# Attention beside the first half of d_ff: TensorE in program order, each product a step behind its inputs, pairs made sooner, partial sums over ScalarE's queue

## The chip, the cores and the metric

The kernel runs on one core of one Trainium2 chip. The metric is device time in microseconds, the median of several executions. TensorE (PE in the profile) multiplies matrices, VectorE (DVE), ScalarE (ACT) and GpSimd (POOL) do the elementwise work, and SyncE (SP) starts nearly all transfers. Each engine works through its own queue in order and waits on semaphores for the others.

## The reference

Three pieces are chained. Sizes: 8 batches, 8 heads, 576 positions, head dimension 64, 32 memory slots; 4608 tokens, d_model 512, d_ff 2048, and 768 for the last piece.

```python
a = exp(phi - max(phi, axis=2)); a = a / (sum(a, axis=2) + 1e-9)     # over the sequence
k_m = einsum('bhsm,bhsd->bhmd', a, k);  v_m = einsum('bhsm,bhsd->bhmd', a, v)
attn = softmax(q @ k_m^T / sqrt(D))                                  # over the 32 memory slots
x = attn @ v_m                                                       # to 4608 x 512
h = x @ w_in;  g = h - tanh(h);  x = g @ w_out                       # 512 -> 2048 -> 512
out = max(x @ w1, x @ w2, x @ w3) @ w_out2                           # 512 -> 768 -> 512
```

## The kernel before

The change touches the first piece and the first half of the second, roughly the first 490 of 1364 us. fp32 products are made of two parts, a high and a low one, so a product is three matmuls (`mm3`).

**The main line.** d_ff is split in 16 chunks of 128, and phase 0 does chunks 0 to 7, phase 1 the others. The list `steps` has one entry for each token tile and chunk: steps 0 to 31 are four tiles of 288 tokens (chunks 0 to 3 of all four, then chunks 4 to 7 of all four), and from step 32 on come tiles of 320, 512 and 320 tokens with eight steps each, so that phase 0 has 104 steps. A step i, in `run`, emits the twelve matmuls of `emit_x(i)` (four output blocks ps_x, gh against wo), after the first block the elementwise work of step i + 3 (`emit_g`: tanh, subtraction, and the split into gh), and after all blocks `emit_h(i + 4)`, the products ps_h. x @ w_in is folded: h is attn times vw, where vw = v_m @ w_in is made for each batch and each quarter of d_ff. When a tile's chunks end, its sums go out of ps_x into xo and to DRAM (xd). For the first four tiles the sums of chunks 0 to 3 are stored, loaded into xo at chunk 4 of the second round, and added to ps_x at chunk 7. xo has a single buffer, and the next tile's first ps_x product waits until its bank has been emptied.

**The side line.** Meanwhile the attention of later batches is made, by generators which `slot()` advances five times in each step, at a fixed rate. `Track fg` holds them in a list, each with a gate, the step from which it may begin. For a batch b there are: `kv_gen` (maxima mx of phi, transposed on TensorE into ps_mx; a diagonal dg multiplied by ones, to spread the maximum; subtraction from phi; Exp; the products ps_kv; n; the transposition ps_t into kT and vT), two `q_gen` (transposes qT of q; products sc; the softmax chain s, st on four engines; aT and at) and two `vw_gen` (products ps_w with vT and wi, cast and subtraction into vw). These eight products a batch share two PSUM banks, m0 and m1, each held until VectorE has taken its contents out. The gates stand relative to `start[0, b]`, the first step that needs the batch (8, 32, 40, 56, 64, 80 and 88 for batches 1 to 7): kv 20 steps ahead, q 16, vw 8 and 6. If `emit_h` needs something that isn't made, `Track.need` runs the list up to it at once.

**The order.** All instructions go through `Paced.call` (line 57 in the profile). The framework's scheduler then places each engine's instructions by its own estimate of time, and not in the order of the code. `behind(ins, mark)` is a bond of order only, without a semaphore: an instruction of the side line stays behind the last tanh, subtraction or x product of the main line that was emitted ahead of it. Transfers go over SyncE's queue, `DMA = nc.sync`.

Of the kernel before, what the change touches and what calls it, by code (L numbers as in the profile page):

```python
# [22 lines left out]
def kernel(  # L23
# [22 lines left out]
    nc = tc.nc  # L46

    class Paced:

        def __init__(self, engine):  # L50
            self.engine, self.mark = engine, None

        def __getattr__(self, name):
            op = getattr(self.engine, name)

            def call(*a, **kw):
                i = op(*a, **kw)  # L57
                if self.mark is not None and background[0]:
                    behind(i.ins, self.mark)
                return i  # L60

            return call
# [20 lines left out]
    LG = 3  # L83
# [146 lines left out]
    def phi_gen(b):  # L230
        load_phi(b)
        ph = phi_t.pop(b)
        yield
        mx = ap.tile([P, H, M], F32, tag="mx", bufs=1, name="mx")
        V.tensor_max(mx, ph[:, :, 0], ph[:, :, 1])
        for c in range(2, C):
            V.tensor_max(mx, mx, ph[:, :, c])
        yield
        pm = bank(1, [P, 2, 2, P], "ps_mx")
        for i in range(2):  # L240
            T.transpose(pm[:, 0, i], mx[:, 4 * i:4 * i + 4].rearrange("p h m -> p (h m)"), ident)
        mt = ap.tile([P, 2], F32, tag="mt", bufs=1, name="mt")
        V.tensor_reduce(mt, pm[:, 0], axis=AX.X, op=ALU.max)
        yield
        dg = ap.tile([P, 2, P], F32, tag="mx", bufs=1, name="dg")
        V.tensor_tensor(out=dg, in0=ident[:, None, :].to_broadcast([P, 2, P]), in1=mt[:, :, None].to_broadcast([P, 2, P]), op=ALU.mult)
        T.matmul(pm[:, 1].rearrange("p i j -> p (i j)"), ones, dg.rearrange("p i j -> p (i j)"), start=True, stop=True)
        yield
        freed[1] = V.tensor_tensor(out=ph, in0=ph, in1=pm[:, 1].rearrange("p i (h m) -> p (i h) m", m=M)[:, :, None, :].to_broadcast([P, H, C, M]), op=ALU.subtract).ins
        yield  # L250
        S.activation(ph, ph, AF.Exp)
        yield
        ph_t[b] = ph
        yield

    vT = [wi_p.tile([P, HP, M], F32, name=f"vT{b}") for b in range(B)]
    kT = {}
# [2 lines left out]
    def kv_mm(b):  # L260
        ph = ph_t.pop(b)
        ps = bank(0, [P, 2, 256], "ps_kv")
        t = kv_t.pop(b)
        for e in range(2):
            for c in range(C):
                pk = P if c < 4 else 64
                for r in range(HP):
                    T.matmul(ps[32 * r:32 * r + 32, e, 2 * D:2 * D + 1], ph[:pk, 2 * r + e, c], ones[:pk, :1], start=c == 0, stop=c == C - 1)
            for c in range(C):
                pk = P if c < 4 else 64  # L270
                for r in range(HP):
                    T.matmul(ps[32 * r:32 * r + 32, e, :2 * D], ph[:pk, 2 * r + e, c], t[:pk, :, 2 * r + e, c], start=c == 0, stop=c == C - 1)
                if c % 2:
                    yield
            yield
        if b:
            load_phi(b + 1)
            load_kv(b + 1)
        rc = ap.tile([P, 2], F32, tag="rc", bufs=2, name="rc")
        V.tensor_scalar(rc, ps[:, :, 2 * D], 1e-9, None, ALU.add)  # L280
        V.reciprocal(rc, rc)
        n = ap.tile([P, 2, 2, D], F32, tag="kvn", bufs=2, name="n")
        V.tensor_tensor(out=n.rearrange("p i e d -> p e i d"), in0=ps[:, :, :2 * D].rearrange("p e (i d) -> p e i d", i=2),
                        in1=rc[:, :, None, None].to_broadcast([P, 2, 2, D]), op=ALU.mult)
        yield
        pt = bank(0, [P, 2, P], "ps_t")
        for i in range(2):
            for e in range(2):
                T.matmul(pt[64 * e:64 * e + 64, i], n[:, i, e], ident, start=True, stop=True)
        kT[b] = ap.tile([P, HP, M], F32, tag="kT", bufs=2, name="kT")  # L290
        for i, t in enumerate((kT[b], vT[b])):
            S.copy(t.rearrange("p r m -> p (r m)"), pt[:, i])
        yield
# [8 lines left out]
    def q_gen(b, hfs):  # L302
# [6 lines left out]
        for hf in hfs:  # L309
            qT = []  # L310
            for g in range(2):
                t = ap.tile([P, 2, NH], F32, tag="qT", bufs=2, name="qT")
                V.transpose(out=t, in_=q_t[b, g][:, :, hf * JH:(hf + 1) * JH].rearrange("p r j d -> p r (j d)"))
                qT.append(t)
                yield
            scs = [bank(e, [P, NH], "sc") for e in range(2)]
            small([(scs[e][32 * r:32 * r + 32], kT[b][64 * e:64 * e + 64, r], qT[r // 2][64 * e:64 * e + 64, r % 2])
                   for r in range(HP) for e in range(2)])
# [32 lines left out]
    vw_t = {}  # L351

    def vw_gen(ph, b, fq):
        while 2 * ph + fq not in wi:
            bg.need("wi2")
        t = at_p.tile([P, 2, 2, FQ], F32R, tag="vw", bufs=4, name="vw")
# [66 lines left out]
        yield  # L423


    class Track:
        def __init__(self):
            self.q = []

        def add(self, name, g, gate=-1):  # L430
            self.q.append([name, g, gate])

        def step(self, now):
            if self.q and self.q[0][2] <= now:
                try:
                    next(self.q[0][1])
                except StopIteration:
                    self.q.pop(0)
                    self.step(now)
# [78 lines left out]
    def emit_g(i):  # L518
        ps = h_t.pop(i)
        nt = steps[i][1][1]  # L520
        th = ga_p.tile([P, NT], F32, tag="th", bufs=2, name="th")[:, :nt]
        S.mark = S.activation(th, ps, AF.Tanh).ins
        V.mark = V.tensor_sub(th, ps, th).ins
        gh = ga_p.tile([P, 2, NT], F32R, tag="gh", bufs=4, name="gh")[:, :, :nt]
        S.copy(gh[:, 0], th)
        G.tensor_sub(gh[:, 1], th, f(gh[:, 0]))
        g_t[i] = gh
# [6 lines left out]
    def emit_x(i):  # L534
# [6 lines left out]
            emit_x.ps = [ps_x.tile([P, NT], F32, tag=f"x{dm}", bufs=1, name=f"ps_x{dm}")[:, :nt] for dm in range(KD)]  # L541
        o = slice(t0, t0 + nt)
        add = ph or t0 < NXI and fc >= 4
        if fc == 4 and add or final and not add:
            emit_x.xo = ga_p.tile([P, KD, NT], F32, tag="xo", bufs=1, name="xo")[:, :, :nt]
            if add:
                DMA.dma_start(out=emit_x.xo, in_=xd[0][:, :, o])
        for dm in range(KD):
            T.mark = mm3(emit_x.ps[dm], (wt[:, 0, dm * P:(dm + 1) * P], wt[:, 1, dm * P:(dm + 1) * P]),
                (gh[:, 0], gh[:, 1]), first, final)  # L550
# [7 lines left out]
                emit_g(i + LG)  # L558
            slot()
        if final:  # L560
            DMA.dma_start(out=xd[ph][:, :, o], in_=emit_x.xo)

    hooks = {}

    def run(lo, hi):
        for i in range(lo, hi):
            now[0] = i
            for fn in hooks.pop(i, ()):
                fn()
            emit_x(i)  # L570
# [57 lines left out]
    for ph in range(2):  # L628
        for b in range(B):
# [2 lines left out]
            aq = max([s0 - AHEAD + 4] + [last_u[bb - 3, fq] - LG for fq in range(2) if bb > 2])  # L632
            av0, av1 = (max(s0 - d, last_u[order[2 * bb + fq - 4]] - LG) if bb > 1 else 0 for fq, d in enumerate((8, 6)))
            if ph == 0 and b > 1:
                fg.add("kv", kv_gen(b), s0 - AHEAD)
                fg.add(("q", 0, b, 0), q_gen(b, (0,)), aq)
                fg.add(("q", 0, b), q_gen(b, (1,)), aq)
            if ph:
                fg.add(("q", 1, b, 0), at_load(b), max(aq, s0 - 10))
            if bb > 1:  # L640
                fg.add(("vw", ph, b, 0), vw_gen(ph, b, 0), av0)
                fg.add(("vw", ph, b, 1), vw_gen(ph, b, 1), av1)
        if ph == 0:
# [284 lines left out]
```

## Time and profile before

| | |
|---|---|
| median of 3 runs | 1368.9 us (1366.58 to 1371.0) |
| profiled execution | 1365.75 us, span 1364.0 us, mean granted clock 0.985 |
| TensorE matmuls | 1285.4 us busy, 94% of the span |
| VectorE, ScalarE, GpSimd | 751.2, 507.1 and 531.8 us busy |

The span is from the first to the last instruction that the profiler recorded. The stage of the change lies between 104 and 449 us: at 104 us step 9 begins, at 449 us step 92.

### The profile page before, as it was taken

The page shows a single profiled execution, that of the slowest core. Times are in us where ns is not written, and L with a number is a line of the kernel's source. Part 1 is how long each engine was busy: PE and PEld are TensorE (multiplying, and loading weights), DVE is VectorE, ACT ScalarE, POOL GpSimd, SP SyncE. Part 2 cuts the span into 40 slices and gives each one's busy share as a digit, 9 for nine tenths or more (in the row PEclk, how much of TensorE's full clock was granted, in tenths as well). Part 3 has the DMA queues.
Part 4 walks back from the last instruction along what each step waited for, and adds up shares of the span by engine and source line. Part 5 has one row for each costly group of instructions (what it writes and reads, how often), then busy time and mean ns, then how long its engine had stood idle before and what let it go on. Part 6 is the DMA issues. An engine that isn't in the chain of part 4 may idle for free.

```text
span 1364.0 us, 22739 instructions
## 1 busy us (share of the span) xinstructions
PE 1285.4 (94%) x8996; PEld 1157.4 (85%) x8996; DVE 751.2 (55%) x1189; ACT 507.1 (37%) x993; POOL 531.8 (39%) x470
## 2 busy tenths in 40 slices
PE   3578898999998999999999999999999999999998
PEld 1457696897897799898989999999999899999996
DVE  3868557666545755756643344555734546457342
ACT  2446244454334455555544332223322323233221
POOL 1637334554423546776754341132311312223110
PEclk9989998999999899999999999999999999999999
DMA  8874847866714536667575139838557477385431
GB/s 204 243 194 127 207 139 189 215 213 172 186 57 178 189 105 236 242 206 251 207 254 168 50 125 364 342 126 307 192 171 286 141 270 268 97 307 197 166 132 47
DMA packets 188394, 264.94 MB, mean 194 GB/s; under 512 B 94976, under 2 KB 160512, under 8 KB 179200
## 3 DMA queue, kind: packets, MB, share of 16 engines
q1 hardware_dynamic: 188000, 259.82, 58.3%
q0 software_dynamic: 288, 3.67, 0.7%
q8 instruction: 71, 1.16, 0.4%
q14 instruction: 35, 0.29, 0.1%
HBM read 199.49 MB, written 63.96 MB: 193 GB/s over the span
## 4 chain that ended last, share of the span: by engine, by line
PE 84%; DVE 7%; SPq 3%; issue 2%; POOL 2%; ACT 1%; DMA 1%; POOLq 0%; ACTq 0%; DVEq 0%
PE b L57 40%; PE ps_x L57 26%; PE ps_h L57 13%; PE ps_w L57 2%; PE ps_kv L57 2%; DVE cvb L57 2%; SPq L224 1%; DVE st L57 1%; DVE s L57 1%; POOL s L57 1%; DVE mx L57 1%; DMA raw<-in_moe_w_out_dram 1%; SPq L214 1%; DVE th L57 1%; DVE vw L57 0%
## 5 line engine op out<-in xcount | busy, mean ns | idle before, releaser
L57 PE MATMUL ps_x<-gh,wo 128*128 128x320 f32 (+2 forms) x2400 | 451.9, 335 | 7.2 <-DVE xo L57 5.5
L57 PEld LDWEIGHTS ps_x<-gh,wo 128*128 128x128 f32 x2400 | 381.4, 191 | 54.7 <-issue 22.9
L57 PE MATMUL b<-mv,sw 128*128 128x384 f32 x2268 | 401.6, 338 | 0.0
L57 PEld LDWEIGHTS b<-mv,sw 128*128 128x128 f32 x2268 | 399.1, 188 | 1.4 <-DMA sw<-sw_d 0.3
L57 POOL TENSOR_TENSOR gh<-th,gh 128x320 fp32r<-128x320 f32 (+2 forms) x200 | 209.8, 1051 | 259.0 <-ACT gh L57 248.9
L57 PE MATMUL ps_h<-at,vw 128*128 128x256 f32 (+2 forms) x1536 | 254.9, 307 | 20.4 <-DVE th L57 10.0
L57 PEld LDWEIGHTS ps_h<-at,vw 128*128 128x128 f32 x1536 | 227.7, 197 | 47.7 <-DVE th L57 15.6
L57 DVE TENSOR_TENSOR th<-ps_h,th 128x320 f32<-128x320 f32 (+2 forms) x200 | 106.7, 536 | 184.2 <-ACT th L57 183.5
L57 ACT ACTIVATE th<-ps_h 128x320 f32<-128x320 f32 (+2 forms) x200 | 95.2, 478 | 200.2 <-PE ps_h L57 185.7
L57 PE MATMUL b<-wz,mh 128*128 128x512 f32 x648 | 150.4, 390 | 1.1 <-DVE ob L57 1.1
L57 PEld LDWEIGHTS b<-wz,mh 128*128 128x128 f32 x648 | 121.3, 188 | 26.5 <-DVE ob L57 2.0
L57 ACT CAST gh<-th 128x320 fp32r<-128x320 f32 (+2 forms) x200 | 99.6, 499 | 96.0 <-DVE th L57 83.8
L57 POOL TENSOR_TENSOR c<-c,u 128x384 f32<-128x384 f32 x36 | 36.5, 1015 | 226.6 <-ACT u L57 226.6
L57 ACT COPY p<-b 128x384 f32<-128x384 f32 x108 | 51.8, 479 | 169.6 <-PE b L57 146.4
L57 DVE TENSOR_TENSOR c<-b,u 128x384 f32<-128x384 f32 x72 | 39.9, 554 | 97.0 <-PE b L57 97.0
L57 DVE TENSOR_SCALAR cvb<-cvb 128x512 f32<-128x512 f32 x112 | 69.8, 624 | 29.8 <-ACT cvb L57 27.0
L57 DVE TENSOR_TENSOR m<-c,m 128x768 f32<-128x768 f32 x72 | 69.0, 958 | 5.7 <-DVE c L57 0.9
L57 DVE TENSOR_TENSOR c<-b,p 128x384 f32<-128x384 f32 x72 | 37.7, 554 | 37.7 <-ACT p L57 34.2
L57 DVE TENSOR_TENSOR vw<-ps_w,vw 128x512 fp32r<-128x512 f32 x64 | 41.4, 681 | 22.9 <-ACT vw L57 22.9
L57 POOL TENSOR_TENSOR mv<-xr,mv 128x384 fp32r<-128x384 f32 x30 | 48.9, 1664 | 12.4 <-PE b L57 9.3
L57 POOL TENSOR_TENSOR m<-m,u 128x384 f32<-128x384 f32 x18 | 21.4, 1189 | 81.6 <-ACT u L57 80.2
L57 ACT CAST mh<-m 128x384 fp32r<-128x384 f32 (+1 forms) x54 | 31.8, 620 | 57.1 <-DVE m L57 57.1
(82 smaller groups left out, 1051.5 us busy)
## 6 DMA issues: line engine op xcount, KB each, us to landing
sw<-sw_d SPq DMA_DIRECT2D x52, 1792.0 KB, 7.6
sw_d<-so SPq DMA_DIRECT2D x9, 1792.0 KB, 7.1
raw<-in_moe_w_out_dram SPq DMA_DIRECT2D x22, 512.0 KB, 5.5
qt<-in_q_dram SPq DMA_DIRECT2D x128, 72.0 KB, 3.1
at_d<-at SPq DMA_DIRECT2D x16, 576.0 KB, 3.7
at<-at_d SPq DMA_DIRECT2D x8, 1152.0 KB, 6.3
raw<-in_moe_w_dram SPq DMA_DIRECT2D x18, 512.0 KB, 4.0
out_dram<-ob SPq DMA_DIRECT2D x144, 64.0 KB, 1.7
```

Of the source, the lines that this page charges most:

```text
L57: i = op(*a, **kw)
L214: DMA.dma_start(out=t[:64, i, :, 4], in_=x[b, :, 4 * P:].rearrange("h p d -> p h d"))
L224: q_dma.dma_start(out=t[64 * e + 32 * h:64 * e + 32 * h + 32, r], in_=src[e, h, r])
```

## The change

It has four parts. (1) From step 9 to step 91, `T.strict` puts every TensorE instruction behind the one emitted before it, so TensorE works in the order of the code. (2) A generator of the side line yields `turns(b)` ahead of a product, and `Track.step` then leaves it alone until that many tanh have been emitted: two until step 28, then one, none for batches 0 and 1. (3) The list of the side line is in another order, with other gates: batches come in pairs (2 and 3, 4 and 5, 6 and 7), the second kv of a pair and its first vw ahead of the first batch's second vw, and most gates are the step in which the buffers that are needed come free, instead of a fixed distance ahead of their use. (4) In phase 0 the stores of xo, and the loads of the four tiles' sums, are started from ScalarE's queue. A load is emitted at chunk 5 instead of 4, and behind the last tanh emitted.

```diff
@@ Paced.call
+                if self.strict:
+                    if self.prev is not None:
+                        behind(i.ins, self.prev)
+                    self.prev = i.ins
@@ phi_gen, kv_mm, q_gen, vw_gen: ahead of ps_mx, dg x ones, ps_kv, ps_t, sc and ps_w
-        yield
+        yield turns(b)
@@ Track
+    turn = [0]
+    def turns(b):
+        return 0 if b < 2 else 2 if now[0] < start[0, 2] - 4 else 1
...
-                    next(self.q[0][1])
+                    if self.q[0][3] < turn[0]:
+                        n = next(self.q[0][1])
+                        self.q[0][3] = turn[0] + n - 1 if n else -1
@@ emit_g
+        turn[0] += 1
@@ emit_x
-        if fc == 4 and add or final and not add:
+        if fc == (4 if ph else 5) and add or final and not add:
...
-                DMA.dma_start(out=emit_x.xo, in_=xd[0][:, :, o])
+                d = (DMA if ph else nc.scalar).dma_start(out=emit_x.xo, in_=xd[0][:, :, o]).ins
+                if ph == 0:
+                    behind(d, S.mark)
...
-            DMA.dma_start(out=xd[ph][:, :, o], in_=emit_x.xo)
+            (DMA if ph else nc.scalar).dma_start(out=xd[ph][:, :, o], in_=emit_x.xo)
@@ run
+            T.strict = 8 < i < start[0, B - 1] + 4
@@ the list of the side line
-                fg.add("kv", kv_gen(b), s0 - AHEAD)
+                if b % 2 == 0:
+                    fg.add("kv", kv_gen(b), s0 - AHEAD)
+                    aq = max([s0 - AHEAD] + [last_u[bb - 3, 1] - LG for _ in range(b > 2)])
+                else:
+                    aq = last_u[bb - 3, 1] - LG
+                av0, av1 = (last_u[order[2 * bb + fq - 4]] - LG for fq in range(2))
+                if b % 2:
+                    fg.add(("vw", 0, b - 1, 1), vw_gen(0, b - 1, 1), last_u[order[2 * bb - 5]] - LG)
                 fg.add(("q", 0, b, 0), q_gen(b, (0,)), aq)
                 fg.add(("q", 0, b), q_gen(b, (1,)), aq)
+                fg.add(("vw", 0, b, 0), vw_gen(0, b, 0), av0)
+                if b % 2:
+                    fg.add(("vw", 0, b, 1), vw_gen(0, b, 1), av1)
+                else:
+                    fg.add("kv", kv_gen(b + 1), av0)
```

**Where instructions stand, before and now.** The first place is TensorE where the vw of batch 3 are made; ps_w with vT_92 are their two products, each with all heads. In the kernel before, this is at the end of step 39 (wo_962 and wo_963 are the weights of chunks 6 and 7, and with wo_304 and 512 tokens step 40 begins):

```order
L57 MATMUL ps_x_2149<-gh,wo_963 128x320 x3
L57 MATMUL ps_x_2150<-gh,wo_963 128x320 x3
L57 MATMUL ps_x_2151<-gh,wo_963 128x320 x3
L57 MATMUL ps_x_2152<-gh,wo_963 128x320 x3
L57 MATMUL ps_w<-wi,vT_92 32x512 x8
L57 MATMUL ps_h<-at,vw 128x256 x10
L57 MATMUL ps_w<-wi,vT_92 32x512 x8
L57 MATMUL ps_h<-at,vw 128x256 x2
L57 MATMUL ps_mx<-ident,mx 128x128 x2
L57 MATMUL ps_h<-at,vw 128x256 x12
L57 MATMUL ps_x_2571<-gh,wo_304 128x512
```

Now the same two products stand in steps 36 and 37 (wo_957 and wo_958 are the weights of chunks 4 and 5):

```order
L57 MATMUL ps_x_2049<-gh,wo_957 128x320 x3
L57 MATMUL sc<-qT,kT 32x288 x8
L57 MATMUL ps_x_2050<-gh,wo_957 128x320 x3
L57 MATMUL ps_x_2051<-gh,wo_957 128x320 x3
L57 MATMUL ps_x_2052<-gh,wo_957 128x320 x3
L57 MATMUL ps_h<-at,vw 128x256 x6
L57 MATMUL ps_w<-wi,vT_92 32x512 x8
L57 MATMUL ps_h<-at,vw 128x256 x6
L57 MATMUL ps_x_2049<-gh,wo_958 128x320 x3
L57 MATMUL ps_w<-wi,vT_92 32x512 x8
```

Both products have moved ahead of steps 37 to 39, the first into the middle of the h of step 40 and directly ahead of the half that uses it, and ps_mx of the next batch has gone from here to a place behind both.

The second place is TensorE in step 32 now (wo_304 is the weight of chunk 0); ps_t belongs to batch 3, and ps_w with vT_91 is the second product of batch 2. In the kernel before, this ps_w stands some steps earlier, apart from the h that uses it.

```order
L57 MATMUL ps_x_2049<-gh,wo_304 128x320 x3
L57 MATMUL ps_t<-ident,n 64x128 x4
L57 MATMUL ps_x_2050<-gh,wo_304 128x320 x3
L57 MATMUL ps_x_2051<-gh,wo_304 128x320 x3
L57 MATMUL ps_x_2052<-gh,wo_304 128x320 x3
L57 MATMUL ps_w<-wi,vT_91 32x512 x8
L57 MATMUL ps_h<-at,vw 128x320 x6
```

So ps_w now stands between the last product of step 32 and the h of step 36, which is the first to need its vw.

The third place is the load of xo (L547 before, L561 now) and the store (L561 before, L577 now) around steps 23 to 25. Before, they stand on SyncE's queue:

```order
L561 DMA xd_120<-xo 512x1x288
L224 DMA qt<-in_q_dram 32x18x32 x11
L547 DMA xo<-xd_120 128x4x288
L224 DMA qt<-in_q_dram 32x18x32 x4
L344 DMA at_d_1416<-at 512x1x288
```

Now they stand on ScalarE's queue; the first tanh (th) of these rows is that of step 24, the next those of 25, 26 and 27:

```order
L57 ACTIVATE th<-ps_h 128x288
L57 CAST gh<-th 128x288
L57 ACTIVATE th<-ps_h 128x288
L57 CAST gh<-th 128x288
L57 ACTIVATE th<-ps_h 128x288
L561 DMA xo<-xd_120 128x4x288
L57 CAST gh<-th 128x288
L57 ACTIVATE s<-s 128x576
L57 ACTIVATE th<-ps_h 128x288
L57 CAST gh<-th 128x288
L577 DMA xd_120<-xo 512x1x288
```

The load has left its place behind eleven pieces of q, and now stands behind the tanh of step 26 and ahead of those of 27 and later.

## Rows read from the trace of the kernel before

**Rows 1.** Windows: us, busy time of each engine (matmuls), PEclk, DMA share, GB/s.
```profile
104.00:449.00 345.00, 322.63 (x3095) 274.65 (x3096) 209.39 (x372) 148.43 (x301) 156.91 (x144) 0.97 0.59 168
166.00:172.50 6.50, 5.67 (x30) 3.76 (x31) 5.89 (x15) 1.07 (x2) 1.18 (x1) 0.50 0.76 221
220.50:230.50 10.00, 8.09 (x41) 5.59 (x42) 7.07 (x13) 5.37 (x11) 4.28 (x4) 0.51 0.72 220
320.00:330.00 10.00, 6.97 (x65) 4.25 (x64) 7.65 (x14) 6.17 (x12) 3.62 (x3) 1.00 0.84 203
420.00:430.00 10.00, 6.50 (x54) 4.65 (x47) 5.42 (x11) 5.70 (x11) 4.33 (x4) 0.94 0.63 205
428.50:432.50 4.00, 4.00 (x21) 3.94 (x20) 0.69 (x1) 1.78 (x4) 3.08 (x3) 0.57 0.98 339
```

**Rows 2.** Timeline of TensorE: start, duration, instruction, [idle before it, releaser].
```profile
127.40 0.41 PE L57 MATMUL ps_mx<-ident,mx 128*128 128x128 f32 x2 [1.41 <-DVE mx L57]
...
159.88 2.08 PE L57 MATMUL ps_h<-at,vw 128*128 128x288 f32 x12 [0.77 <-DVE th L57]
166.84 1.06 PE L57 MATMUL ps_x<-gh,wo 128*128 128x288 f32 x3 [4.88 <-DVE xo L57]
...
218.10 1.09 PE L57 MATMUL ps_w<-wi,vT 64*32 64x512 f32 x16 [2.20 <-DVE s L57]
221.09 2.56 PE L57 MATMUL ps_h<-at,vw 128*128 128x256 f32 x10 [1.89 <-ACT vw L57]
...
227.59 0.69 PE L57 MATMUL ps_mx<-ident,mx 128*128 128x128 f32 x2 [1.33 <-DVE vw L57]
...
327.70 0.44 PE L57 MATMUL ps_mx<-ident,mx 128*128 128x128 f32 x2 [1.67 <-DVE vw L57]
...
427.59 3.68 PE L57 MATMUL ps_h<-at,vw 128*128 128x256 f32 x20 [2.21 <-DVE th L57]
```

**Rows 3.** Timeline of SyncE's queue: start, duration, instruction.
```profile
150.95 10.57 SPq L224 DMA_DIRECT2D qt<-in_q_dram  x11
161.56 0.63 SPq L547 DMA_DIRECT2D xo<-xd  x1
```

**Rows 4.** Tile xo from 104 to 449 us, its loads and stores.
```profile
DMA to landing us min/median/max: 3.3/4.1/7.1
```

**Rows 5.** Timeline of TensorE, two starts one step of 288 tokens apart.
```profile
142.96 0.97 PE L57 MATMUL ps_h<-at,vw 128*128 128x288 f32 x6
...
145.35 0.29 PE L57 MATMUL ps_h<-at,vw 128*128 128x288 f32 x1
```

**Rows 6.** VectorE's groups, 104 to 449 us: busy us, mean ns, idle before.
```profile
L57 DVE TENSOR_TENSOR vw<-ps_w,vw 128x512 fp32r<-128x512 f32 x28 | 18.2, 677 | 7.5 <-ACT vw L57 7.5
...
L57 DVE SCALAR_TENSOR_TENSOR cvb<-raw,cvb 128x512 uint32<-128x512 uint32 x15 | 15.1, 1007 | 0.2
L57 DVE TENSOR_TENSOR mx<-mx,phi 128x256 f32<-128x256 f32 x18 | 12.9, 717 | 0.3
L57 DVE TENSOR_SCALAR cvb<-cvb 128x512 uint32<-128x512 uint32 x15 | 11.6, 771 | 0.3
...
L57 DVE TENSOR_SCALAR cvb<-cvb 128x512 f32<-128x512 f32 x15 | 9.6, 637 | 5.2 <-ACT cvb L57 4.7 <-POOL cva L57 0.4
L57 DVE STREAM_TRANSPOSE aT<-s 128x576 f32<-128x576 f32 x12 | 9.3, 776 | 10.1 <-POOL s L57 10.1
L57 DVE TENSOR_TENSOR phi<-phi,ps_mx 128x1280 f32<-128x1280 f32 x6 | 8.9, 1481 | 2.4 <-PE ps_mx L57 2.4
L57 DVE TENSOR_TENSOR xo<-ps_x,xo 128x288 f32<-128x288 f32 x16 | 6.4, 447 | 9.5 <-PE ps_x L57 4.8 <-DMA xo<-xd 4.7
```

**Rows 7.** ScalarE's group of the Exp of phi, 104 to 449 us.
```profile
L57 ACT ACTIVATE phi<-phi 128x1280 f32<-128x1280 f32 x6 | 7.7, 1276 | 4.8 <-DVE phi L57 4.8
```

**Rows 8.** Timeline of ScalarE at the start: two casts of vw.
```profile
83.85 1.07 ACT L57 CAST vw<-ps_w 128x512 fp32r<-128x512 f32 x2 [1.74 <-PE ps_w L57]
```

**Rows 9.** Timeline of TensorE behind these casts.
```profile
86.42 0.72 PE L57 MATMUL sc<-qT,kT 64*32 64x288 f32 x16 [1.40 <-DVE vw L57]
```

More of the change, by code (lines that the diff above doesn't have):

```diff
@@ L50, in __init__ @@
         def __init__(self, engine):
-            self.engine, self.mark = engine, None
+            self.engine, self.mark, self.strict, self.prev = engine, None, False, None
         def __getattr__(self, name):
@@ L243, in phi_gen @@
         V.tensor_reduce(mt, pm[:, 0], axis=AX.X, op=ALU.max)
-        yield
         dg = ap.tile([P, 2, P], F32, tag="mx", bufs=1, name="dg")
         V.tensor_tensor(out=dg, in0=ident[:, None, :].to_broadcast([P, 2, P]), in1=mt[:, :, None].to_broadcast([P, 2, P]), op=ALU.mult)
+        yield turns(b)
         T.matmul(pm[:, 1].rearrange("p i j -> p (i j)"), ones, dg.rearrange("p i j -> p (i j)"), start=True, stop=True)
@@ L251, in phi_gen @@
         S.activation(ph, ph, AF.Exp)
-        yield
+        yield turns(b)
         ph_t[b] = ph
-        yield
     vT = [wi_p.tile([P, HP, M], F32, name=f"vT{b}") for b in range(B)]
@@ L284, in kv_mm @@
                         in1=rc[:, :, None, None].to_broadcast([P, 2, 2, D]), op=ALU.mult)
-        yield
+        yield turns(b)
         pt = bank(0, [P, 2, P], "ps_t")
@@ L315, in q_gen @@
                 yield
+            yield turns(b)
             scs = [bank(e, [P, NH], "sc") for e in range(2)]
@@ L353, in vw_gen @@
     def vw_gen(ph, b, fq):
+        if ph == 0:
+            yield turns(b)
         while 2 * ph + fq not in wi:
@@ L430, in add @@
         def add(self, name, g, gate=-1):
-            self.q.append([name, g, gate])
+            self.q.append([name, g, gate, -1])
         def step(self, now):
@@ L543, in emit_x @@
         add = ph or t0 < NXI and fc >= 4
-        if fc == 4 and add or final and not add:
+        if fc == (4 if ph else 5) and add or final and not add:
             emit_x.xo = ga_p.tile([P, KD, NT], F32, tag="xo", bufs=1, name="xo")[:, :, :nt]
             if add:
-                DMA.dma_start(out=emit_x.xo, in_=xd[0][:, :, o])
+                d = (DMA if ph else nc.scalar).dma_start(out=emit_x.xo, in_=xd[0][:, :, o]).ins
+                if ph == 0:
+                    behind(d, S.mark)
         for dm in range(KD):
@@ L634 @@
             if ph == 0 and b > 1:
-                fg.add("kv", kv_gen(b), s0 - AHEAD)
+                if b % 2 == 0:
[6 more added lines that the diff above has]
+                    fg.add(("vw", 0, b - 1, 1), vw_gen(0, b - 1, 1), last_u[order[2 * bb - 5]] - LG)
                 fg.add(("q", 0, b, 0), q_gen(b, (0,)), aq)
                 fg.add(("q", 0, b), q_gen(b, (1,)), aq)
+                fg.add(("vw", 0, b, 0), vw_gen(0, b, 0), av0)
[3 more added lines that the diff above has]
+                    fg.add("kv", kv_gen(b + 1), av0)
             if ph:
                 fg.add(("q", 1, b, 0), at_load(b), max(aq, s0 - 10))
-            if bb > 1:
                 fg.add(("vw", ph, b, 0), vw_gen(ph, b, 0), av0)
```

## The prediction

> **What bounds the kernel now.** I read the windows first, over the stretch in which the change acts: from step 9, at 104 us, to step 92, at 449 us. TensorE is busy for 322.6 of these 345 us [rows 1], so all that a better order can save there is 22.4 us of idle time, and what a lowered clock costs. Both lie in few places. The windows around 325 and 425 us hold 3.0 and 3.5 us of idle time, though ScalarE and VectorE have work for only 5 to 8 us of each ten. In three windows the granted clock is near 0.5 or 0.57, so TensorE runs partly or wholly at 1.2 GHz instead of 2.4 [rows 1]. A matmul at half clock takes twice as long, so a window costs its busy time times the missing share: 5.67 × 0.50 = 2.8 us around 170, 8.09 × 0.49 = 4.0 us around 225, and 4.00 × 0.43 = 1.7 us around 430 us. Each of the three falls stands right behind waits of TensorE.
>
> Next I read TensorE's own timeline at these places, for what it waited for [rows 2]. There are four kinds. (a) The first transposes of batch 2 (ps_mx) wait 1.4 us for VectorE's maxima. (b) At 166.84, in step 24, the input product of partial sums waits 4.9 us for VectorE's additions into xo, after a wait of 0.8 for a late subtraction in the step before, which I count with it. (c) At 218 to 228, in steps 39 and 40, a pair's ps_w, its h and the following ps_mx wait 2.2, 1.9 and 1.3 us. (d) At 327.70 and 427.59 what stands behind two later pairs waits 1.7 and 2.2 us. A bank of m0 or m1 is held there until VectorE has taken its contents out, and vw is asked for the moment that it is made.
>
> For (b), SyncE's queue says what was late [rows 3]: the load of xo leaves at 161.56, behind eleven pieces of q that took the queue 10.57 us to issue. From there to the product that waits it is 166.84 − 161.56 = 5.3 us.
>
> **The change, part by part.**
> *Sums over ScalarE's queue.* The four loads no longer stand behind q's pieces, but the load for step 24 now stands behind the tanh of step 26 (the order shows this), which runs at the start of step 23. A step of 288 tokens takes 145.35 − 142.96 = 2.4 us [rows 5]. With 0.5 us for the tanh, as an estimate, and the 5.3 from issue to product, the product can start at 5.8, where it would be due at 2.4: a wait of 3.4 us in place of 4.9 + 0.8. That gains 2.3 us. A load or store of xo lands in 3.3 to 7.1 us, 4.1 in the middle [rows 4], so the wait lies between 2.6 and 6.4. I take the clock fall behind it (2.8) as staying, since a wait of 3.4 remains. The Trainium skill (DMA: Bandwidth & Descriptors, Issuing engines are not separate DMA queues) says that transfers started by different engines share the same 16 DMA engines, and that another issuer saves only the time to start them, usually little. By that rule alone step 24 would gain nothing and the sum below would be 2.3 us higher, near 1366.8. Here the time to start them was itself the trouble: 10.57 us of issuing ahead of one load.
>
> *Program order and one step between input and product.* A product no longer stands on TensorE until its turn has come, and no later work can go ahead of it. In (a), ps_mx stands a whole step later, so its 1.4 us go. In (d), the second pair of vw for batches 4 and 6 comes several steps earlier, so the idle time of both windows goes, 3.0 + 3.5, and so does the clock fall behind the second, 1.7. Sum: −9.6 us. The bounds are nothing (the waits turn up elsewhere, a rival) and all of it.
>
> In (c), sc and ps_w of batch 3 keep nearly their distance: the order shows a pair of ps_w right behind the first half of h(40) in step 36. I keep its first two waits, 2.2 and 1.9, and halve the third, since ps_mx now stands two steps later: 4.8 instead of 5.4, a gain of 0.6. The bounds are 1.9 and 7.6, one wait alone or every wait with half as much again. The fall (4.0) stays.
>
> *What is new.* Where work is in order and not yet ready, TensorE now stands still. I looked for the products whose VectorE or ScalarE work cannot end in time, by adding the means [rows 6, 7] between two subtractions of tanh.
> Step 28: the order has four maxima, aT, two vw and three additions to xo between two subtractions, 4 × 0.72 + 0.78 + 2 × 0.68 + 3 × 0.45 = 6.4 us, where two steps give 4.8. I take 1.4 for the rest (0 to 4), as the first of the additions frees the first bank early.
> Step 32: the second ps_w of batch 2 is forced out directly ahead of the h that uses it. The copy and the subtraction of one half are 0.53 + 0.68 = 1.2 us [rows 6, 8], and with 0.5 for what the engines are in at that time it is 1.7. The bounds are 0.7 and 3.0, the latter as two halves and hand-overs.
> Step 47: ps_mx of batch 5 shares a bank with vw of batch 4. Between two subtractions VectorE has four maxima, aT, two vw and three passes of a weight's splitting (0.64 + 0.77 + 1.01), 7.4 us, against some two steps of 320 tokens. I take 2.0 (1 to 3).
> The other products, some 44, have a step between input and use. The longest chain is phi's: 1.48 on VectorE and 1.28 on ScalarE [rows 6, 7], 2.8 us where the shortest step gives 2.4. Most steps are longer, so I take 0.05 for each, 2.0 us in all (0 to 11, below).
>
> *The start.* Before step 9, two copies of xo and a store now stand ahead of the casts of vw on ScalarE; TensorE already waits 1.4 us for that vw [rows 9]. Two copies are about 2 × 0.45, as VectorE's operations on such a tile [rows 6], and one issue about 0.6 [rows 3], 1.5 in all; some of it lies beside the ps_w that the casts wait for anyway, so I take 1.0 (0 to 2.2). After step 92 the order of every engine is as before, so those stages cost nothing and give nothing.
>
> *Sum.* Gains: 2.3 + 9.6 + 0.6 = 12.5. Losses: 1.4 + 1.7 + 2.0 + 2.0 + 1.0 = 8.1. Net −4.4 us against the profiled execution of 1365.75 us, which is 1361.35. The median of the runs is 1368.9, a factor of 1.0023 above it, so **1364.5 us**, 0.32% less. A change of 0.3% is about what a measurement of this kernel can tell from none.
>
> **The rivals.**
> *A clean success.* The step between input and product does what it can: the new waits halve (−4), (c) halves too (−2.4) and, without its waits, has no clock fall (−4.0). Net −14.8, so 1354.0 us. For it speaks the stretch's many steps without any wait: TensorE's idle time sits in so few places that most products have slack now. Against it: (c) hangs on a chain through three engines that is as long as before.
> *Slower: one step is too short.* TensorE's free order now lets other matmuls run while a product's input is late; in strict order each late input is TensorE's own idle time. It decides above 0.15 us for each of 44 products (then −4.4 + 44 × 0.10 = 0). At 0.30 each, 0.25 more than I counted, 11 us come onto the sum: +6.6, which is 1375.5 us. For it: phi's chain of 2.8 us against a step of 2.4, and VectorE and ScalarE, each with its own order. Against it: most steps are of 320 or 512 tokens.
> *Slower: the transfers hold ScalarE.* Each store waits for four additions and each load for the landing of the store before it, and behind both stands a tanh. From a store to the load behind it are 4.1 us of landing [rows 4] against 2.4 of a step; the h that needs the bank which this tanh empties comes two steps on, 4.8 us [rows 5], and less some 1.7 for tanh, subtraction and h's own place (an estimate) the lead is 3.1. If each of four tiles loses 2 us beyond that lead, the sum is +3.6, so 1372.5 us; it decides from 1.1 us each. The Trainium skill (TensorE: Matmul & The Clock Gate, Architectural detail: the array is 16× 32×32, not 1× 128×128) calls ScalarE's queue strictly first in, first out, which would hold a tanh behind such a transfer. No row shows a transfer on ScalarE's queue before.
> *The waits only move.* What (a), (b) and (d) give comes back at the next product in order, because the chains through three engines, and not the order, set the total of idle time. Net 0, 1368.9 us. For it: the stages without idle time have little left to hide a chain in. Against it: the three engines besides TensorE are at most three quarters busy in the windows of (d) [rows 1].
>
> **How the numbers follow.** Chances: the forecast 0.42, clean success 0.22, steps too short 0.15, ScalarE held 0.09, waits only move 0.12. The forecast's own range, from 1360 to 1369, comes from the bounds of steps 24, 28 and 36; its middle stands at the edge of 0.3%, so 0.24 of its 0.42 count as faster and 0.18 as the same. Faster: 0.24 + 0.22 = 0.46. The same: 0.18 + 0.12 = 0.30. Slower: 0.15 + 0.09 = 0.24. The range 1350 to 1375 leaves out the slower half of the slow cases (0.12) and the best third of clean success (0.07).
>
> **What would show it.** In the changed profile: the windows around 325 and 425 us of before without idle time; the wait for xo's additions near step 24 at 3.4 us with a fall of the clock behind it; ps_w and h in step 36 with 4 to 5 us of waits and a fall; waits of 1 to 2 us at steps 28, 32 and 47. The sum is wrong if idle time between 104 us and the end of step 92 differs by more than 4 us from 22.4 − 10.8 + 7.1 = 18.7 us (10.8 of the gains are idle time, 1.7 the clock's), or if ScalarE's tanh waits behind a transfer.

## The result, and the profile after

The changed kernel is slower: 1378.49 us median (6 runs, 1375.9 to 1381.28) against 1370.94 us for the kernel before in the same setting (6 runs, 1366.58 to 1371.07), a ratio of 1.0066 with a 95% interval of 1.0048 to 1.0083. The prediction of 1364.5 us and its range up to 1375 are both below it. The profiled execution has a span of 1374.1 us, 10.1 more than before.

First the windows by stage, in the changed kernel: steps 0 to 8, 9 to 43, 44 to 59, 60 to 91, 92 to 103 (columns as in [rows 1]), then one window in the middle of the third stage. A stage begins here with the tanh that its first step emits, which is the tanh of three steps on. By this measure step 9 begins at 113.7 us in the kernel before; at the 104 us named above, TensorE is still in the products of step 8.

```profile
58.60:116.00 57.40, 42.49 (x401) 33.32 (x402) 41.88 (x66) 23.36 (x49) 27.83 (x25) 0.76 0.73 203
...
116.00:260.70 144.70, 129.90 (x1339) 109.18 (x1338) 92.30 (x166) 58.38 (x122) 60.99 (x60) 0.95 0.58 164
260.70:334.50 73.80, 64.59 (x574) 52.18 (x573) 45.65 (x80) 33.25 (x67) 39.37 (x35) 0.93 0.73 204
334.50:462.50 128.00, 127.14 (x1148) 108.36 (x1147) 66.81 (x116) 53.12 (x103) 48.92 (x43) 1.00 0.42 130
...
462.50:504.90 42.40, 39.56 (x249) 33.78 (x247) 24.29 (x37) 18.92 (x41) 19.68 (x19) 1.00 0.47 156
...
324.50:331.30 6.80, 5.56 (x30) 3.89 (x31) 3.81 (x8) 3.41 (x7) 6.00 (x6) 0.50 0.86 183
```

The same stages of the kernel before, by its own times of these tanh:

```profile
58.80:113.70 54.90, 40.81 (x416) 32.07 (x417) 41.22 (x66) 23.38 (x50) 28.62 (x26) 0.88 0.77 209
...
113.70:256.30 142.60, 127.73 (x1327) 108.61 (x1327) 86.85 (x161) 58.35 (x123) 62.21 (x60) 0.94 0.61 169
256.30:311.40 55.10, 55.10 (x523) 48.20 (x522) 38.14 (x68) 27.93 (x60) 33.40 (x30) 1.00 0.73 210
311.40:449.70 138.30, 131.77 (x1196) 111.14 (x1195) 76.31 (x134) 57.39 (x110) 53.76 (x47) 0.99 0.49 145
...
449.70:494.80 45.10, 42.28 (x249) 35.45 (x247) 24.41 (x37) 18.93 (x42) 19.61 (x19) 0.92 0.44 147
```

The length less PE's busy time is TensorE's idle time. The stages before step 44 are 2.5 and 2.1 us longer. Their sum, 4.6, is firmer than its two parts, since TensorE had done 416 matmuls at the end of the first stage before, and has done 401 now. The last is 2.7 shorter, though the order there is the same: a stretch at 1.2 GHz that the profile before has there is missing (it is missing too in the kernel before with the splitting moved, below, and there again in the fastest kernel, so I don't credit it to the change). The largest part of the loss, 8.4 us, lies in steps 44 to 91. The two middle stages differ in which products stand in which, so they are read together: 73.8 + 128.0 = 201.8 us against 55.1 + 138.3 = 193.4. Steps 60 to 91 have lost their idle time (6.5 to 0.9 us), as was forecast, but steps 44 to 59 had none and now have 9.2, and a part of it runs at 1.2 GHz: the window from 324.5 costs 5.56 × 0.50 = 2.8 us.

TensorE's timeline names the places (start, duration, instruction, [idle before it, releaser]):

```profile
130.23 0.41 PE L57 MATMUL ps_mx<-ident,mx 128*128 128x128 f32 x2 [0.15 <-DVE mx L57]
...
163.73 2.92 PE L57 MATMUL ps_x<-gh,wo 128*128 128x288 f32 x12 [3.16 <-DVE xo L57]
...
178.20 0.67 PE L57 MATMUL ps_x<-gh,wo 128*128 128x288 f32 x3 [0.70 <-DVE xo L57]
...
180.98 0.96 PE L57 MATMUL ps_x<-gh,wo 128*128 128x288 f32 x3 [1.16 <-DVE xo L57]
...
217.05 1.09 PE L57 MATMUL ps_w<-wi,vT 64*32 64x512 f32 x16 [1.78 <-DVE s L57]
220.15 2.17 PE L57 MATMUL ps_h<-at,vw 128*128 128x256 f32 x6 [2.01 <-ACT vw L57]
...
230.37 0.44 PE L57 MATMUL ps_mx<-ident,mx 128*128 128x128 f32 x2 [1.70 <-DVE vw L57]
...
277.24 0.69 PE L57 MATMUL ps_mx<-ident,mx 128*128 128x128 f32 x2 [2.84 <-DVE vw L57]
...
310.85 1.26 PE L57 MATMUL sc<-qT,kT 64*32 64x288 f32 x16 [1.45 <-DVE qT L57]
...
325.74 1.96 PE L57 MATMUL ps_w<-wi,vT 64*32 64x512 f32 x16 [4.31 <-DVE vw L57]
```

They stand in steps 14, 24, 28 (two), 36 (two), 38, 47, 55 and 58. The first is what is left of (a), the second is (b) with 3.16 us where 3.4 was forecast, the waits in steps 36 and 38 are (c) with 5.5 against 4.8. The worst is new. In step 58 the second ps_w of batch 5 waits 4.3 us, because the first, one step ahead of it, still holds the two banks: VectorE's second subtraction of its vw ends at 325.69, and the waiting ps_w starts at 325.74.

How a product one step ahead can still hold its bank is best seen at step 47. VectorE there, in the changed kernel:

```profile
269.46 0.49 DVE L57 TENSOR_TENSOR th<-ps_h,th 128x320 f32<-128x320 f32 x1 [1.01 <-ACT th L57]
269.86 0.46 DVE L57 TENSOR_SCALAR cvb<-cvb 128x512 f32<-128x512 f32 x1
270.24 1.40 DVE L57 TENSOR_TENSOR mx<-phi 128x256 f32<-128x256 f32 x1
271.57 0.77 DVE L57 STREAM_TRANSPOSE aT<-s 128x576 f32<-128x576 f32 x1
272.26 0.41 DVE L57 TENSOR_SCALAR cvb<-cvb 128x512 uint32<-128x512 uint32 x1
272.59 0.41 DVE L57 TENSOR_TENSOR mx<-mx,phi 128x256 f32<-128x256 f32 x1
272.93 0.68 DVE L57 SCALAR_TENSOR_TENSOR cvb<-raw,cvb 128x512 uint32<-128x512 uint32 x1
273.53 1.65 DVE L57 TENSOR_TENSOR mx<-mx,phi 128x256 f32<-128x256 f32 x1
275.10 0.68 DVE L57 TENSOR_TENSOR vw<-ps_w,vw 128x512 fp32r<-128x512 f32 x1
275.70 0.88 DVE L57 TENSOR_TENSOR mx<-mx,phi 128x256 f32<-128x256 f32 x1
276.51 0.68 DVE L57 TENSOR_TENSOR vw<-ps_w,vw 128x512 fp32r<-128x512 f32 x1
277.11 0.47 DVE L57 TENSOR_TENSOR th<-ps_h,th 128x320 f32<-128x320 f32 x1
```

The ps_w of this vw ran on TensorE from 269.44 to 270.53. Its two subtractions stand behind maxima, aT and three passes of the weights' splitting (cvb), without a gap in between, and end at 277.19. The same bank's next product, ps_mx, starts at 277.24.

### The profile page after: what moved, and what is told of

Read it like the earlier page. It is cut to its first block, busy times and chain, and to the rows that moved or that the text cites. A ratio compares the mean times of both kernels' runs of the same rounds, so it can differ in the third digit from the quotient of the medians.

```text
span 1374.1 us, 22724 instructions
## 1 busy us (share of the span) xinstructions
PE 1290.0 (94%) x8996; PEld 1158.0 (84%) x8996; DVE 755.9 (55%) x1189; ACT 508.1 (37%) x993; POOL 531.0 (39%) x470
## 4 chain that ended last, share of the span: by engine, by line
PE 77%; DVE 9%; DMA 5%; SPq 3%; ACT 2%; issue 2%; POOL 2%; ACTq 0%; DVEq 0%; POOLq 0%
PE b L57 39%; PE ps_x L57 22%; PE ps_h L57 11%; DVE cvb L57 2%; PE ps_kv L57 2%; SPq L228 2%; PE ps_w L57 2%; DVE mx L57 1%; DMA raw<-in_moe_w_out_dram 1%; DMA xd<-xo 1%; DVE st L57 1%; DVE s L57 1%; SPq L218 1%; DVE th L57 1%; DMA xo<-xd 1%
## 5 line engine op out<-in xcount | busy, mean ns | idle before, releaser
L57 PE MATMUL ps_x<-gh,wo 128*128 128x320 f32 (+2 forms) x2400 | 464.8, 338 | 8.3 <-DVE xo L57 6.5
L57 PE MATMUL ps_h<-at,vw 128*128 128x256 f32 (+2 forms) x1536 | 250.1, 305 | 17.3 <-DVE th L57 7.4
L57 POOL TENSOR_TENSOR m<-m,u 128x384 f32<-128x384 f32 x18 | 21.4, 1190 | 82.2 <-ACT u L57 80.8
```

## The experiments

Ratios are to the kernel before, run beside it on the same chip, with 95% intervals.

**What each part does alone.** Without part 1 (`T.strict = False`):

```diff
-            T.strict = 8 < i < start[0, B - 1] + 4
+            T.strict = False
```

> The change without part 1: TensorE's order is again the scheduler's. Theory: most of the loss is TensorE standing still at the few products whose inputs are late (4.3 us in step 58, 2.8 in step 47, 2.2 in step 28, with clock falls of 2.8, 1.5 and 1.7 us behind them) and some 3 us of longer busy time in strict order; free, other matmuls fill these places, so 8 to 13 us come back and the ratio to the kernel before is 0.997 to 1.001. Rival: the list with its gates and spacing makes the products late whatever the order, or ScalarE's queue is the cause; then it stays at 1.005 to 1.007.

Measured: 1.0083 (1.0060 to 1.0105). The rival holds: free to reorder, TensorE still waits, 4.6 us for ps_mx at 238 us for example, and the time is not better. Program order is not what costs the time here. TensorE's timeline of this run:

```profile
238.37 0.69 PE L57 MATMUL ps_mx<-ident,mx 128*128 128x128 f32 x2 [4.60 <-DVE vw L57]
```

Without part 4 (the branches of `emit_x` as before, all on `DMA`, loads at chunk 4):

```diff
-        if fc == (4 if ph else 5) and add or final and not add:
+        if fc == 4 and add or final and not add:
...
-            (DMA if ph else nc.scalar).dma_start(out=xd[ph][:, :, o], in_=emit_x.xo)
+            DMA.dma_start(out=xd[ph][:, :, o], in_=emit_x.xo)
```

> The change without part 4: stores and loads of xo go over SyncE's queue as before, the loads at chunk 4. Theory: ScalarE's queue costs about 2.7 us at the start (steps 0 to 9) and saves about as much at step 24, so the ratio stays near 1.006 (1.004 to 1.008). Rival: transfers on ScalarE's queue hold tanh and are the main cause; then it falls to 1.000.

Measured: 1.0065 (1.0044 to 1.0086), as the theory had it. And part 4 alone, on the kernel before (the same lines the other way round):

> The kernel before with part 4 alone: stores and loads of xo of phase 0 over ScalarE's queue. Theory: plus 2 to 3 us in steps 0 to 9, minus 2 to 3 at step 24, so the ratio is 0.999 to 1.001. Rival: the transfers on ScalarE's queue are the main cause, 1.004 or more.

Measured: 0.9993 (0.9980 to 1.0006). ScalarE's queue neither costs nor gives.

Without part 2 (`turns` gives 0), and part 1 alone on the kernel before:

```diff
-        return 0 if b < 2 else 2 if now[0] < start[0, 2] - 4 else 1
+        return 0
```

> The change without part 2: no product waits for a step to pass since its inputs were emitted, so in program order each stands right behind them. Theory: the spacing does what it is for, and without it TensorE waits for nearly each of some 44 products, 0.5 to 1 us each: plus 20 to 40 us on the changed kernel, ratio 1.02 to 1.035. Rival: the spacing is itself the loss, by making the later products late; then 1.000 or below.

> The kernel before with part 1 alone: TensorE in program order from step 9 to 91, without spacing, old list. Theory: each product is late by what its inputs need, as in the run without spacing: ratio 1.02 to 1.035. Rival: the order of the code is near the scheduler's anyway; then 1.000 to 1.005.

Measured: 1.0298 (1.0275 to 1.0322) and 1.0343 (1.0326 to 1.0360). Program order without the step between input and product costs 39 and 47 us over the kernel before; with it, this is gone. So the two belong together, and the step does nearly all that was hoped of it.

Without part 3 (the list and the gates of the kernel before):

> The change without part 3: list and gates as before, in program order and with the spacing. Theory: what costs time is a second vw one step behind the first, whose banks are not yet free; by the order this stands in steps 60 and 61 and again in 84 and 85 (the changed kernel has it in 57 and 58, without a wait in 80 and 81), so one or two waits of some 4 us with clock falls of some 3 us: ratio 1.005 to 1.010. Rival: the list is the loss; then 1.000 to 1.002.

Measured: 0.9999 (0.9988 to 1.0010). This refutes my theory of the moment, that any second vw one step behind the first must wait: with the old list this pair stands in steps 60 and 61, one step apart, and the second has no wait. But it clears the rest: with the old list, the other three parts together cost nothing, so the loss came with the new list. (The new list with none of the other parts was not run.) Nor is one step of distance free with the old list: ps_mx in step 62, one step behind the second ps_w of that pair, waits 1.6 us. TensorE's timeline there, then VectorE's:

```profile
331.24 0.44 PE L57 MATMUL ps_mx<-ident,mx 128*128 128x128 f32 x2 [1.62 <-DVE vw L57]
```

```profile
326.10 0.41 DVE L57 TENSOR_TENSOR mx<-phi 128x256 f32<-128x256 f32 x1
326.55 3.44 DVE L57 TENSOR_TENSOR mx<-mx,phi 128x256 f32<-128x256 f32 x3
329.90 1.28 DVE L57 TENSOR_TENSOR vw<-ps_w,vw 128x512 fp32r<-128x512 f32 x2
```

VectorE makes the four maxima ahead of the two subtractions here; no pass of the weights' splitting stands among them.

**Where the new list loses.** One step more ahead of each second vw:

```diff
-            yield turns(b)
+            yield turns(b) + (fq if b > 1 else 0)
```

> The change with one step more ahead of the second vw of each batch from 2 on (two steps between the pair of products that share the banks). Theory: the wait of 4.3 us in step 58 and the clock fall of 2.8 behind it go, the ratio falls by 0.004 to 0.005, to about 1.002. Rival: the wait only moves to the next product or to the h that needs this vw; then 1.005 to 1.007.

Measured: 1.0003 (0.9988 to 1.0017), so some 8 us come back. All products behind the first such pair also move one or two steps later, so the run doesn't say which of them paid. With the gate of one product alone moved:

```diff
-                fg.add(("vw", 0, b, 0), vw_gen(0, b, 0), av0)
+                fg.add(("vw", 0, b, 0), vw_gen(0, b, 0), 59 if b == 5 else av0)
```

> The change with the gate of one product moved: the first vw of batch 5 from step 48 to step 59, so that the pair stands in steps 60 and 61 instead of 57 and 58. All before step 57 is as in the changed kernel. Theory: the loss of the new list lies mainly in this pair, which comes so soon behind the batch's second sc that ScalarE's cast still stands behind the softmax: 7 us go, ratio 1.001 to 1.003. Rival: the run with every second vw later gained elsewhere (steps 47 to 56); then 1.004 to 1.007.

Measured: 1.0039 (1.0029 to 1.0050). The pair of batch 5 is worth some 3.7 us, about half of what I expected and of what the run before gave, and the interval still touches that of the changed kernel. The waits of steps 47 and 55 stayed (2.7 and 1.6 us); step 24 waits 5.1 us in this profile, 2 more than in the changed kernel, which may hide a part of the gain.

Then the splitting of weights was moved, with TensorE's order left alone:

```diff
-        bg.add("wos", wo_store(fc), start[0, 2])
+        bg.add("wos", wo_store(fc), start[0, 5] - 2)
```

> The change with the splitting of the other eight weight blocks (cva, cvb, cs) begun at step 62 instead of 32; TensorE's order stays the same up to step 92. Theory: what makes the products of steps 47, 55 and 58 late is that VectorE and ScalarE do the splitting between them; without it these waits (2.8, 1.5 and 4.3 us) and their clock falls (4.2) mostly go, and the splitting beside steps 62 to 92 brings at most half of that back: ratio 0.998 to 1.002. Rival: the softmax alone holds the cast, and the waits stay: 1.004 to 1.008.

Measured: 1.0001 (0.9989 to 1.0013). The window of steps 44 to 59 in this run:

```profile
258.10:318.80 60.70, 59.99 (x574) 49.19 (x573) 37.39 (x67) 25.96 (x54) 24.94 (x25) 1.00 0.61 155
```

The same 574 matmuls take 60.7 us instead of 73.8, with 0.7 us idle and no fall of the clock, and all three waits of steps 47, 55 and 58 are gone. VectorE in place of the long row above:

```profile
267.16 0.42 DVE L57 TENSOR_TENSOR mx<-phi 128x256 f32<-128x256 f32 x1
267.61 3.01 DVE L57 TENSOR_TENSOR mx<-mx,phi 128x256 f32<-128x256 f32 x3
270.54 1.28 DVE L57 TENSOR_TENSOR vw<-ps_w,vw 128x512 fp32r<-128x512 f32 x2
```

Without cvb, and with aT already done at 266.6, the subtractions of vw end at 271.8, just ahead of the next product at 271.9. The gain is not kept whole: where the splitting now runs, another ps_mx one step behind a ps_w waits, in step 70 (TensorE's timeline of this run):

```profile
369.18 0.69 PE L57 MATMUL ps_mx<-ident,mx 128*128 128x128 f32 x2 [3.59 <-DVE vw L57]
```

So the waits of 3 to 4 us for a bank stand where two things meet: one step of distance, and the splitting in the same steps. For a shorter wait one step is enough, as the run with the old list showed. To take both apart, two products of batch 7 got two steps on top of this:

```diff
-        yield turns(b)
+        yield turns(b) + (b == B - 1)
         pm = bank(1, [P, 2, 2, P], "ps_mx")
@@ vw_gen
-            yield turns(b)
+            yield turns(b) + (fq if b == B - 1 else 0)
```

> As the run with the splitting begun at step 62, and two steps instead of one ahead of batch 7's first transposes and of its second vw, the two products that waited there (3.6 us with a clock fall of 3.0, and 1.5 us). Theory: a product waits only where the splitting and a distance of one step meet; both are gone now from step 44 on, so 5 to 8 us go and the ratio is 0.994 to 0.997. Rival: with the splitting beside it two steps are too short as well, or another product waits: 0.999 to 1.002.

Measured: 0.9979 (0.9967 to 0.9992), 1367.33 us: 0.2% faster than the kernel before, and faster than the changed one, though less than expected. Its windows for steps 44 to 59 and 60 to 91:

```profile
260.20:321.00 60.80, 60.09 (x574) 49.25 (x573) 37.41 (x67) 26.00 (x55) 24.98 (x25) 1.00 0.60 154
321.00:453.70 132.70, 129.63 (x1157) 110.22 (x1156) 83.62 (x142) 65.39 (x126) 71.56 (x60) 1.00 0.60 195
```

Together 193.5 us, what the kernel before takes (193.4), with 3.8 us idle and the full clock. So the loss of these stages is gone, but no gain stands in its place, and where the 0.2% come from its profile doesn't show (span 1366.3 us, against 1364.0 in the profile before). The kernel before with the splitting moved in the same way:

> The kernel before with the splitting begun at step 62 instead of 32, nothing else. Theory: its free order lets other matmuls run where a product is late, and its list has no product one step behind another but the pairs, so only the waits around 325 us (3.0) may go and those around 425 us grow: ratio 0.998 to 1.002. Rival: the splitting costs the kernel before as much as the changed one, 0.992 to 0.996.

Measured: 1.0015 (1.0000 to 1.0030), so no gain there: in this order and list, where the splitting runs is not what costs time. Why it hurts the changed kernel and not this one was not shown. It is not the fixed order alone, since the waits stayed when TensorE was free to reorder; my reading is that the new list puts products closer behind one another.

One step instead of two between input and product in the early steps of 288 tokens (with the later second vw):

```diff
-        return 0 if b < 2 else 2 if now[0] < start[0, 2] - 4 else 1
+        return 0 if b < 2 else 1
```

> The change with one step more ahead of the second vw, and with one step instead of two between input and product in steps 9 to 27. By the order batch 3's vw then stand in steps 29 and 31 instead of 37 and 38. Theory: the waits of 5.5 us and the clock fall of 2.4 in steps 36 to 39, and those of 1 in step 32, go, and the short steps before 28 bring back some 3 us: ratio 0.994 to 0.998. Rival: a step of 288 tokens is too short for a product's inputs, and every product of steps 13 to 31 waits: 1.000 to 1.005.

Measured: 1.0053 (1.0036 to 1.0069). The waits of steps 32 to 39 fell to 1.2 us in all, but three new long ones, of 6.1, 2.8 and 4.1 us in steps 19, 22 and 28, came in their place. Of these short steps the rival is right.

**The wait in step 24.** The load was put ahead of the tanh of step 25, in the kernel with the later second vw:

```diff
         S.mark = S.activation(th, ps, AF.Tanh).ins
+        if i == 25:
+            behind(S.mark, early[0])
```

> The change with one step more ahead of the second vw, and with the load of xo for step 24 put ahead of the tanh of step 25 instead of behind that of 26. Theory: the store before it has landed by then, so the load leaves some 4 us sooner, and the wait of 4.3 us in step 24 and the clock fall of 2.9 us behind it go: ratio 0.995 to 0.997. Rival: the load holds ScalarE while it waits for the store, or the wait moves to the additions of the next tile; then 1.000.

Measured: 1.0023 (1.0010 to 1.0037), no better than without it (1.0003, 0.9988 to 1.0017). ScalarE's timeline in this run:

```profile
159.31 0.58 ACTq L563 DMA_DIRECT2D xo<-xd  x1
159.99 0.71 ACT L57 ACTIVATE th<-ps_h 128x288 f32<-128x288 f32 x2 [6.53 <-DMA xd<-xo]
```

The load waits for the landing of the store ahead of it, and holds two tanh for 6.5 us. It leaves no sooner than before. In the changed kernel the store (L577) goes out at 149.58 and the load at 158.74, in the moment of its landing. The tanh ahead of the load starts there at 158.28, so its place in the queue would let it leave little sooner. In the run with the later second vw the two come apart: the tanh starts at 158.02, the store of 149.32 lands 10.0 us later, and the load leaves at 159.36, with the landing. ScalarE's timeline of the changed kernel:

```profile
149.58 0.54 ACTq L577 DMA_DIRECT2D xd<-xo  x1
...
158.74 0.57 ACTq L561 DMA_DIRECT2D xo<-xd  x1
```

Tile xo of the changed kernel from 149 to 150.2 us, where this store is its only transfer:

```profile
DMA to landing us min/median/max: 9.1/9.1/9.1
```

And the window between store and load in the changed kernel, the last two numbers being DMA share and GB/s:

```profile
149.60:159.00 9.40, 9.40 (x85) 8.48 (x84) 5.67 (x11) 3.17 (x9) 2.50 (x4) 1.00 1.02 314
```

The store needs 9.1 us to land, because the DMA engines are full (share 1.02) with phi, k and v of the next batch, whose loads left SyncE's queue from 145.7 us on. To test this, those loads were moved to step 24, in the fastest kernel so far:

```diff
-        if b:
+        if b and b != 2:
             load_phi(b + 1)
             load_kv(b + 1)
...
+    hooks[24] = [lambda: load_phi(3, S.mark), lambda: load_kv(3, S.mark)]
     run(0, start[0, 2])
```

> As the run with the splitting later and the two gaps, and with the loads of phi, k and v of batch 3 begun at step 24 instead of step 20. Theory: the wait in step 24 is neither the queue's nor the load's own. The store ahead of the load takes 9 us to land instead of 4, because these loads fill the DMA engines (busy share 1.02 from 149.6 to 159 us in the changed kernel); moved, the store lands in some 4 us, the load leaves 5 us sooner, and the wait (3.2 to 5.6 us in the runs so far) and its clock fall (1.7 to 2.9 us) go: ratio 0.992 to 0.995. Rival: phi, k or v then come too late for steps 28 to 31, or crowd the next store: 0.997 to 1.001.

Measured: 1.0032 (1.0019 to 1.0045). Tile xo in this run from 146 to 152 us has two transfers, the store at 147.01 and the load behind it:

```profile
DMA to landing us min/median/max: 3.3/3.7/4.2
```

The load's own landing is the 4.2, so the store landed in 3.3 us. The load left in that moment, at 150.31, and step 24 has no wait: how long the store takes to land is shown as a cause of the wait. It is not the only change, since the load also stands two tanh earlier in ScalarE's queue than in the changed kernel, and the early landing would be of little use without that. But the moved loads, with q's pieces behind them, now fill the engines under the next store, at 158.78, which took 10.1 us. The load behind that one left only at 173.62, 4.7 us after the landing; ScalarE stood still for 7.3 us until then, and the profile names a piece of q as what released it, which was not taken apart. Step 28 waits longer than step 24 ever did (TensorE's timeline of this run):

```profile
179.65 1.78 PE L57 MATMUL ps_x<-gh,wo 128*128 128x288 f32 x6 [10.04 <-DVE xo L57]
```

## Why the prediction was wrong

**The step that failed** is "the other products, some 44, ... I take 0.05 for each, 2.0 us in all". The timeline has 4.3 us in step 58 alone, 1.5 in step 55, and about 0.5 each for ps_kv in steps 31, 49 and 72: 7.4 in sum. A mean over 44 products was the wrong form. Nearly all wait for nothing; a few that meet the weights' splitting one step behind another product wait for 3 to 4 us. I saw one of these (step 47: 2.0 forecast, 2.84 measured) and did not look for others of the same kind, though the order showed both ps_w of batch 5 one step apart in steps 57 and 58.

**What was left out** are falls of the clock behind the new waits. I priced the falls that go, but none that come. The one at 324.5 us costs 2.8, and those behind steps 47 and 28 are each half as long; together about 6 us. Their windows:

```profile
276.70:280.10 3.40, 2.86 (x8) 2.39 (x9) 2.68 (x5) 1.30 (x3) 2.10 (x2) 0.50 1.03 344
181.10:184.50 3.40, 3.40 (x15) 3.38 (x16) 0.58 (x2) 0.87 (x2) 0.80 (x1) 0.51 0.94 331
```

Other falls shrank or are missing, so the net is less. By the windows of the stages, busy time times the missing share of the clock is about 10.2 us before step 9 (before the change 4.9), 6.5 in steps 9 to 43 (7.7), 4.5 in steps 44 to 91 (1.3) and nothing after step 92 (3.4): some 4 us more in all.

**The prediction's own test** says the same. It allowed 4 us around 18.7 us of idle time from step 9 to step 91. The three stages above hold 14.8 + 9.2 + 0.9 = 24.9 us, more than those of the kernel before (21.4).

**The gains came mostly as forecast.** (a) fell from 1.41 to 0.15 us. Of (d), the window around 425 us lost its idle time and its fall; the one around 325 lost its wait, and the wait of step 58 stands a few steps earlier in its place, so I read these 3.0 us as a wait that moved. (c) stayed: 5.5 us against 4.8, with a fall of the clock behind it that costs 2.6 instead of 4.0.

**Step 24** was right in its size, 3.16 against 3.4, and only half right in its cause. In the kernel before, q's pieces were the limit, as I read [rows 3]: the store at 149.8 took 7.1 us and had landed at 156.9, and the load left at 161.56. In the changed kernel the load does stand behind the tanh of step 26, as forecast, but the store ahead of it lands only in the same moment, 9.1 us after its start. The prediction has no term for that landing, so that the size came out is in part luck. In the runs that share this piece of order the wait was 3.2 to 5.6 us. The rule of the Trainium skill (DMA: Bandwidth & Descriptors, Issuing engines are not separate DMA queues), by which another issuer gains little, came out right for the total: the change without part 4 is at 1.0065, and part 4 alone at 0.9993.

**The new waits that I named** were of the right order: step 28 2.2 us (1.4), step 32 0.9 (1.7). The start cost 2.5 against 1.0 us in this profile, at a lower granted clock (0.76 against 0.88). One profile doesn't give it, though: in the other runs that share this start it takes 55.2 to 57.8 us, and 55.9 in the kernel before with the splitting moved, against 54.9 in the profile before. In the run of part 4 alone it cost 0.6.

**The rivals.** "One step is too short" named the direction and came within 3 us of the time, but by a spread over all products that isn't there. "The transfers hold ScalarE" did not happen in the change, where no tanh waits for a transfer, and happened as described when the load was moved ahead: 6.53 us, which agrees with the Trainium skill (TensorE: Matmul & The Clock Gate, Architectural detail: the array is 16× 32×32, not 1× 128×128), by which ScalarE's queue is strictly first in, first out. "Waits only move" fits one half of (d), the 3.0 us around 325 us.

**What stays open:** The terms above don't add up to the whole miss, 14.5 us from the forecast −4.4 to the 10.1 that the profiled execution lost. TensorE's busy time in the page is 1290.0 us against 1285.4; by the sum above, the stretches at half clock explain most of that. Why moving the pair of batch 5 alone gives only half of what one step more gives everywhere was not settled either.

## What to carry to other kernels

Program order and spacing between a product and its inputs are one change: the order alone cost 3.4% here, with spacing nothing. A schedule is only as good as its worst places, so look, product by product, at what else the engine that must empty its bank does in those very steps, instead of taking a mean wait; and price the stretch at the lower clock behind the longer waits as well. Where a load waits for a store, look at when the store lands and what fills the DMA engines then, before moving the load to another queue or ahead.

## What the runs showed of the hardware that was not expected

An instruction of VectorE on two SBUF operands took four times as long beside one of GpSimd. In VectorE's rows of step 47 above, the same operation on mx takes 0.41 us at 272.59 and 1.65 at 273.53, and GpSimd's timeline has an instruction beside the second one and nothing beside the first:

```profile
271.32 1.06 POOL L57 TENSOR_TENSOR gh<-th,gh 128x320 fp32r<-128x320 f32 x1
273.12 1.77 POOL L57 TENSOR_TENSOR at<-aT,at 128x576 fp32r<-128x576 f32 x1 [0.74 <-ACT at L57]
274.86 1.44 POOL L57 TENSOR_TENSOR cva<-cvb,cva 128x512 uint32<-128x512 uint32 x1
```

The slow one ends at 275.18, soon after GpSimd's ends at 274.89, and the subtraction of vw, which reads one operand from PSUM, takes 0.68 us beside GpSimd's work at 275.10 as anywhere. This agrees with the Trainium skill (SBUF — State Buffer, Who interferes with whom): a VectorE instruction with two SBUF inputs contends with a GpSimd instruction that reads SBUF, and one with at most one SBUF input, outside VectorE's two-port modes, doesn't. The GpSimd instruction beside the slow maximum belongs to the attention (at), not to the splitting; beside cva, which does, the next maximum took 0.88 us. So the splitting makes a product late by its own passes on VectorE, and by a smaller part through GpSimd.
